# Spreading the weight rounding of a fused HGRN2 and serf-MLP kernel: load order, rounding rate and activation steps of the first turns

## The chip, the cores and the metric

The kernel runs on one core of a Trainium2 chip. The metric is the device time of one execution in microseconds, the median of three runs. The profile is of one execution of the same program. Engines are named as in the profile: PE is TensorE, DVE VectorE, ACT ScalarE, POOL GpSimd, SP the engine that issues most of the DMAs.

## The reference

The first part is a gated linear recurrence over 768 time steps for 4 batches and 8 heads of width 48. The second part is a two-layer MLP over the 3072 tokens, with the activation h * erf(softplus(h)).

```python
f = 1.0 / (1.0 + np.exp(-f_logit))
for t in range(S):                       # S = 768
    state = f[:, :, t, :, None] * state + np.einsum('bhd,bhe->bhde', k[:, :, t], v[:, :, t])
    y[:, :, t] = np.einsum('bhd,bhde->bhe', q[:, :, t], state)
x = y.transpose(0, 2, 1, 3).reshape(B * S, H * D)      # 3072 x 384
h = x @ w_in                                           # 384 x 2048
sp = np.maximum(h, 0.0) + np.log1p(np.exp(-np.abs(h)))
out = (h * erf(sp)) @ w_out                            # 2048 x 384
```

The two weight matrices come as 64-bit floats; everything else is 32-bit.

## The kernel before

**Tiling.** The sequence is cut into 24 chunks of 128 time steps (6 for each batch), and two chunks make a block of 256 tokens, so there are 12 blocks. A chunk `g` goes through four stages. `stage_d` (L381) sums the log decays with one matmul, takes two exponentials on ACT, sends eight small DMAs that put the chunk's total decays into `Tall` (L398, from chunk 3 on), and scales q and k on DVE into `qd` and `kd` (L402, L406). `stage_t` (L410) transposes both on PE and copies them out of PSUM on ACT, and releases the state update that the chunk before had left over (`late`). `stage_s` (L450) makes the scores and the state products on PE, masks the scores (on DVE for chunks 0 to 2, L503; on ACT and POOL from chunk 3 to 9, L495 and L498) and updates the state on DVE (`next_state`, L443 to L446). `stage_y` (L511) forms the output of the chunk on PE and copies it on ACT into `xT`, the input of the MLP (L536). `clamp` (L357, DVE) and `logs` (L363, ACT) prepare a block's decays ahead of its `stage_d`; `prepare` is both in a row.

**MLP.** `hidden(blk, gi)` (L585) makes one of four groups of 512 hidden columns of a block: 12 steps of one fp32 matmul each, which PE carries out as two, and one eviction on ACT (L601). `activate` (L546) is a generator of ten steps for each group. Step 1 is an exponential, 2 and 3 are two tanh (all ACT), 4 and 5 two products on DVE (L165), then three empty steps, 9 a last tanh (ACT, L566), 10 a product (DVE, L568). `act_step` (L574) advances each running group by one step and starts the next group five steps after the one before, so that two run at once. The tiles `e` and `x` have two buffers each. `project_first` (L673) and `project` (L701) are the second matmul; the later one uses seven products in place of eight, with sums made on DVE (`sum_w`, `sum_h`).

**Rounding.** The 64-bit weights are loaded raw in 16 pieces of 768 KB, eight of `w_in` and eight of `w_out`, into places that are still free: `w_out_sb`, the ring `Hg` of hidden groups, and `scratch` (`HOMES`, L264). `round_piece` (L295) turns a piece into 32-bit floats with one ACT operation (L311) and six DVE operations (L313, L317, L322, L326, L331, L336). `weights_step` (L851) issues one DVE operation of the piece in work; the ACT operation of the next piece goes out ahead of L331. So a piece takes six steps. `load_more` (L868) loads a further piece of `w_out` when the piece that had its place before has been rounded. A matmul with a piece's weights waits for that piece's L336: `hidden(blk, gi)` needs pieces 2 gi and 2 gi + 1.

**Order of the work.** The order on every engine is written out by hand (`tc.manual_schedule`): each engine carries out its instructions in the order in which the program issues them. A front part (L819 to L919) brings chunks 0 and 1 through all stages and chunk 2 through the first two. Then come 12 turns (`for it in range(n_blocks)`, L937). A turn has slots: in each slot `slots(it)` issues one matmul step of the MLP, and the loop body adds to it what is due. These are rounding steps from the accumulator `due` (L955), a further load (L959), a stage of the recurrence when the slot is in the list `at` (L961), clamp and logs of a later block, and an activation step (L984 to L995). Turn 1 (`it == 0`) has 96 slots: the hidden groups of blocks 0 and 1, in the order of block and group 0.0, 0.1, 1.0, 0.2, 1.1, 0.3, 1.2, 1.3. Turn 2 has 48 slots (block 2). Turn 3 has 80 (block 3, then the second matmul of block 0). Turn 4 begins with the second matmul of block 1.

```python
due += (1 if s < 42 else 0.6 if s < 72 else 0.3) if it == 0 else 0.42 if it == 1 else 0.6
while due >= 1:
    weights_step()
    due -= 1
```

Of the kernel before, what the change touches and what calls it, by code (L numbers as in the profile page):

```python
# [74 lines left out]
def kernel(  # L75
# [21 lines left out]
    CPB = 2  # L97
# [131 lines left out]
    def load(g, what="qkv", queue=None):  # L229
        b, c = divmod(g, NCH)  # L230
        queue = queue or nc.sync
        for src, t, n in ((q, qns[g % NQ], "q"), (k, kns[g % NQ], "k")):
            if n in what:
                queue.dma_start(out=t[:].rearrange("t (h d) -> t h d", d=D), in_=heads(src, b, c))
        if "v" in what:
            queue.dma_start(
                out=vts[g % NV][:].rearrange("t (h d) -> t h d", d=D), in_=heads(v, b, c)
            )
# [40 lines left out]
    def load_piece(i):  # L279

        assert home_free(i)
        n = d_ff // n_pieces
        if i < n_pieces:
            dst = w_in_sb[:, :, bass.ts(i, n)]
        else:
            m = n_ft // n_pieces
            j = i - n_pieces
            dst = w_out_sb[:, bass.ts(j, m), :]
        raw = None if wpe == 1 else raw_home(i).bitcast(U32)
        to = dst if wpe == 1 else raw.rearrange("p (t w) -> p t w", t=dst.shape[1])  # L290
        src = w_in[:, bass.ts(i, n * wpe)] if i < n_pieces else w_out[bass.ts(j, m * P), :]
        nc.sync.dma_start(out=to, in_=src.rearrange("(t p) w -> p t w", p=P))
        raws[i] = (dst, raw)
# [63 lines left out]
    def clamp(blk, j0, j1):  # L357
        lt = lts[blk][:, j0:j1, :].rearrange("t j c -> t (j c)")
        nc.vector.tensor_scalar(
            out=lt, in0=lt, scalar1=LOGIT_MIN, scalar2=None, op0=ALU.max  # L360
        )

    def logs(blk, j0, j1):  # L363

        lt = lts[blk][:, j0:j1, :].rearrange("t j c -> t (j c)")
        use_exp_ln()
        nc.scalar.activation(out=lt, in_=lt, func=AF.Exp, scale=-1.0)
        nc.scalar.activation(out=lt, in_=lt, func=AF.Ln, bias=1.0)

    def prepare(*which):  # L370
        clamp(*which)
        logs(*which)
# [444 lines left out]
    with tc.manual_schedule():  # L817
# [5 lines left out]
        load(0, "kv", nc.scalar)  # L823
        load(0, "q")
        load_f(1)
        load(1, "qk")
        load_f(2)
        load_piece(0)
        load(1, "v")
        load(2)  # L830
        load_piece(1)
        load_piece(2)
        load_f(3)
        nc.gpsimd.memset(tri[:], 1.0)
# [45 lines left out]
        def weights_steps(n):  # L880
            for _ in range(n):
                weights_step()
# [5 lines left out]
        keep_busy(6)  # L888
        prepare(0, 1, 2)
        stage_t(0)  # L890
        load(3, "qk")
        load_piece(3)
        stage_d(1)
# [42 lines left out]
        due = 0.0  # L936
        for it in range(n_blocks):  # L937
            gen, n = slots(it)
            if it == 0:
                todo = [(stage_s, 2), (stage_y, 2), (stage_d, 3), (stage_t, 3), (stage_s, 3), (stage_y, 3),  # L940
                        (stage_d, 4), (stage_t, 4), (stage_d, 5), (stage_s, 4), (stage_t, 5),
                        (stage_y, 4)] + stages(2)[4:]
                at = [1, 5, 6, 12, 16, 23, 34, 42, 48, 52, 60, 74, 76, 80, 88, 94]
            else:
                todo = stages(it + 2) if it + 2 < n_blocks else []
                at = [n * x // 48 for x in (2, 6, 11, 17, 25, 29, 34, 41)] if it == 1 else [int(3 + (n - 13) / max(1, len(todo)) * i) for i in range(len(todo))]
            if ADJACENT <= it + 2 < n_blocks:

                at = [0, 1, 15, 24, 31, 52, 66] if it + 2 == ADJACENT else [2, 26, 42, 54, 76, 90]
                at = at[: len(todo)]  # L950
            if it + 3 < n_blocks:
                prepare_at = at[todo.index((stage_d, (it + 3) * CPB))] - 14
            at, todo = deque(at), deque(todo)
            for s, _ in enumerate(gen):
                due += (1 if s < 42 else 0.6 if s < 72 else 0.3) if it == 0 else 0.42 if it == 1 else 0.6  # L955
                while due >= 1:
                    weights_step()
                    due -= 1
                if s % 6 == 3:  # L959
                    load_more()  # L960
                if at and s == at[0]:  # L961
                    at.popleft()
                    f, g = todo.popleft()
                    f(g)
                    if f in (stage_y, stage_y_s):
                        if g + NSV < n_chunks:
                            load_sv(g + NSV)
                        load_to(g + LOOK)
                        if g == 2:
                            load(5, "v")  # L970
                            load_piece(7)
                if it == 0 and s == 14:
                    prepare(2, 0, CPB)
                if it == 0 and s == 9:
                    load_f(6)
                    load_f(7)
                if s == n // 2 and it + 4 < n_blocks:
                    for j in range(CPB):
                        load_f((it + 4) * CPB + j)
                if it + 3 < n_blocks and s == prepare_at - 6:  # L980
                    clamp(it + 3, 0, CPB)
                if it + 3 < n_blocks and s == prepare_at:
                    logs(it + 3, 0, CPB)
                if it < 2:  # L984
                    step = it == 1 and s % 6 == 3
                elif it == 2:
                    step = s % 5 in (1, 3)
                elif it == 3:
                    step = s % 7 in (1, 4)
                elif it == n_blocks - 1:  # L990
                    step = s % 3 == 1
                else:
                    step = s % 9 in (2, 6)
                if step:
                    act_step()  # L995
                if it == 2:
                    if s % 2:
                        sum_step()
                elif it > 2:
                    if s == n - n_h and it < n_blocks - 1:  # L1000
                        to_sum.extend(sum_h(groups[it - 1, gi]) for gi in range(NS))
                    if it == n_blocks - 1 and s % n_o == 40 and s < 2 * n_o:
                        blk = n_blocks - 2 + s // n_o
                        to_sum.extend(sum_h(groups[blk, gi]) for gi in range(NS))
                    if it == 3:
                        if s % 2:
                            sum_step()
                    elif s < n_o or s % 3 == 0 or it == n_blocks - 1:
                        sum_step()
                if it == n_blocks - 2 and s in (5, 40):  # L1010
                    next(check)
            assert not todo
# [214 lines left out]
```

## Time and profile before

| | before |
|---|---|
| time, median of 3 (lowest to highest) | 618.1 us (617.54 to 618.85) |
| profiled span | 616.6 us |
| PE busy | 588.3 us (95%) |
| weight loads on PE | 514.5 us (83%) |
| DVE busy | 459.7 us (75%) |
| ACT busy | 382.9 us (62%) |
| POOL busy | 14.9 us (2%) |
| mean granted PE clock | 0.985 |
| HBM read, written | 35.59 MB, 4.72 MB |

The table of stages, the chain of waits and the timelines are read in the prediction. In the timeline a line gives the start, the duration from the first start to the last end, engine, line, operation and tiles, the number of instructions merged into it, and in brackets how long the engine was idle before it and what released it. In the list of waits a line names who waited, for whom, how many us in total, how many times, and the longest. A busy PE is not PE at its peak, since the ends of matmuls are modelled and the clock varies; the granted clock stands beside it in the table of stages.

### The profile page before, as it was taken

The numbers are of one execution on the slowest core, as the hardware profiler recorded it, in microseconds if no ns is written. First come the engines' busy times: TensorE is split into PE (matmuls) and PEld (weight loads), VectorE is DVE, ScalarE is ACT, GpSimd is POOL, SyncE is SP. The second block draws the span as 40 slices with busy tenths as digits, with TensorE's granted clock in tenths as the row PEclk, the third lists the DMA queues.
The fourth block names the chain that finished last, engine by engine and source line by source line (L and its number), as shares of the span: only waits on it lengthen the run. The fifth ranks groups of instructions, "written<-read, shape, count | busy, mean of one in ns | idle before, by whom it ended". The sixth has DMA issues, their size and how long they took to land.

```text
span 616.6 us, 13769 instructions
## 1 busy us (share of the span) xinstructions
PE 588.3 (95%) x5729; PEld 514.5 (83%) x5729; DVE 459.7 (75%) x785; ACT 382.9 (62%) x483; POOL 14.9 (2%) x33
## 2 busy tenths in 40 slices
PE   8778799999999999999999999999999999999996
PEld 7556688887655689989989988988988989989996
DVE  4898998697489597896896875896886795656651
ACT  5735365987875678875866585875775666366000
POOL 1000011010000000000000000000000000000000
PEclk9987899999999999999999999999999999999999
DMA  9998753441241222133133132042130000000000
GB/s 201 248 228 208 199 175 63 71 88 17 53 77 28 41 63 52 25 81 54 33 71 53 32 73 53 14 91 53 15 65 15 3 27 0 28 1 0 27 27 30
DMA packets 155604, 41.36 MB, mean 67 GB/s; under 512 B 147344, under 2 KB 150416, under 8 KB 155536
## 3 DMA queue, kind: packets, MB, share of 16 engines
q1 hardware_dynamic: 153312, 39.82, 29.6%
q8 instruction: 47, 0.77, 0.5%
q10 hardware_dynamic: 2224, 0.59, 0.4%
q14 instruction: 21, 0.17, 0.1%
HBM read 35.59 MB, written 4.72 MB: 65 GB/s over the span
## 4 chain that ended last, share of the span: by engine, by line
PE 74%; DVE 11%; ACT 8%; DMA 3%; issue 2%; SPq 1%; POOL 0%; DVEq 0%; ACTq 0%; POOLq 0%
PE hps L594 31%; PE ops L735 25%; PE ops L684 7%; PE y L532 3%; PE ps_t L418 3%; PE ps_d L387 2%; ACT x L160 2%; PE sc L467 1%; PE sc L475 1%; DVE sv L445 1%; DVE sv L446 1%; DVE w_in_sb L322 1%; DVE Hg L568 1%; DVE w_in_sb L336 1%; PE busy L379 1%
## 5 line engine op out<-in xcount | busy, mean ns | idle before, releaser
L594 PE MATMUL hps<-xT,w_in_sb 128*128 128x256 f32 x1152 | 264.7, 386 | 5.0 <-DVE w_in_sb L336 2.9
L594 PEld LDWEIGHTS hps<-xT,w_in_sb 128*128 128x128 f32 x1152 | 218.5, 193 | 39.2 <-ACT xT L536 2.8
L165 DVE SCALAR_TENSOR_TENSOR e<-x,e 128x1024 f32<-128x1024 f32 x96 | 117.1, 1220 | 13.2 <-ACT x L160 12.6
L160 ACT ACTIVATE x<-Hg,serf_bias 128x1024 f32<-128x1024 f32 x88 | 97.5, 1140 | 0.2
L157 ACT ACTIVATE e<-Hg 128x1024 f32<-128x1024 f32 x44 | 46.5, 1058 | 61.7 <-DVE Hg L568 57.6
L735 PE MATMUL ops<-wT,Hg 128*128 128x192 f32 x320 | 78.4, 328 | 0.0
L568 DVE TENSOR_TENSOR Hg<-Hg,e 128x1024 f32<-128x1024 f32 x44 | 53.7, 1222 | 22.6 <-ACT e L566 22.5
L735 PE MATMUL ops<-wT,scratch 128*128 128x192 f32 x288 | 67.8, 326 | 0.9 <-DVE scratch L743 0.9
L735 PE MATMUL ops<-w_out_sb,Hg 128*128 128x192 f32 x320 | 65.1, 326 | 0.0
L601 ACT COPY Hg<-hps 128x1024 f32<-128x1024 f32 x44 | 44.4, 1010 | 32.7 <-PE hps L594 32.4
L735 PEld LDWEIGHTS ops<-wT,Hg 128*128 128x128 f32 x320 | 55.7, 190 | 1.9
L735 PEld LDWEIGHTS ops<-w_out_sb,Hg 128*128 128x128 f32 x320 | 54.6, 190 | 2.0
L566 ACT ACTIVATE e<-e 128x1024 f32<-128x1024 f32 x48 | 50.3, 1048 | 1.9 <-DVE e L165 1.8
L735 PEld LDWEIGHTS ops<-wT,scratch 128*128 128x128 f32 x288 | 50.2, 190 | 1.1 <-issue 1.1
L503 DVE TENSOR_TENSOR qA<-sc,tri 64x256 f32<-64x256 f32 x68 | 28.7, 422 | 27.3 <-PE sc L475 26.3
L743 DVE TENSOR_TENSOR scratch<-scratch,ops 128x384 f32<-128x384 f32 (+1 forms) x41 | 20.3, 494 | 29.5 <-ACT scratch L751 23.0
L532 PEld LDWEIGHTS y<-qA,sv 128*32 128x32 f32 x1536 | 24.9, 113 | 19.6 <-issue 12.4
L532 PE MATMUL y<-qA,sv 128*32 128x64 f32 x1536 | 29.9, 226 | 10.9 <-issue 5.1
L425 ACT COPY qA<-ps_t 64x512 f32<-64x512 f32 x48 | 27.7, 577 | 19.4 <-PE ps_t L418 19.0
L402 DVE TENSOR_TENSOR qd<-qn,dp 128x384 f32<-128x384 f32 x24 | 13.4, 556 | 33.6 <-ACT dp L390 33.5
L735 PE MATMUL ops<-w_out_sb,scratch 128*128 128x192 f32 x144 | 34.7, 326 | 0.0
L445 DVE TENSOR_TENSOR sv<-sc,sv 48x192 f32<-48x192 f32 x80 | 28.3, 354 | 8.3 <-ACT qA L495 6.9
(111 smaller groups left out, 648.1 us busy)
## 6 DMA issues: line engine op xcount, KB each, us to landing
lt<-in_f_logit_dram SPq DMA_DIRECT2D x24, 192.0 KB, 3.7
qn<-in_q_dram SPq DMA_DIRECT2D x24, 192.0 KB, 3.4
kn<-in_k_dram SPq DMA_DIRECT2D x23, 192.0 KB, 3.7
vt<-in_v_dram SPq DMA_DIRECT2D x23, 192.0 KB, 3.7
out_dram<-scratch SPq DMA_DIRECT2D x11, 384.0 KB, 2.6
sv<-in_v_dram SPq DMA_DIRECT2D x84, 48.0 KB, 2.8
w_out_sb<-in_moe_w_in_dram SPq DMA_DIRECT2D x4, 768.0 KB, 6.1
Hg<-in_moe_w_in_dram SPq DMA_DIRECT2D x4, 768.0 KB, 6.6
```

Of the source, the lines that this page charges most:

```text
L157: nc.scalar.activation(out=dst[:], in_=h, func=AF.Exp)
L160: nc.scalar.activation(out=dst[:], in_=h, func=AF.Tanh, bias=serf_bias[:, i : i + 1], scale=SERF_KAB[i][0])
L165: nc.vector.scalar_tensor_tensor(out=e[:], in0=x[:], scalar=SERF_KAB[i][2], in1=e[:], op0=ALU.add, op1=ALU.mult)
L445: nc.vector.tensor_tensor(out=new, in0=add, in1=old, op=ALU.add)
L503: nc.vector.tensor_tensor(out=qA[half(1 - r), r, :, half(c)], in0=sc[half(c), r], in1=tri1[half(c)].unsqueeze(1).broadcast_to((C, HP, C)), ...
L532: nc.tensor.matmul(y[M * i : M * (i + 1), kt, half(c)], lhsT=sv[:, r, c, a, o : o + M], rhs=qA[:, r, a, half(c)], start=(n == 0), stop=Tru ...
L566: nc.scalar.activation(out=e[:], in_=e[:], func=AF.Tanh, scale=SERF_C)
L568: nc.vector.tensor_tensor(out=h, in0=h, in1=e[:], op=ALU.mult)
L594: nc.tensor.matmul(hps[:, j, :], lhsT=w_in_sb[:, kt, ft * P : (ft + 1) * P], rhs=xTs[blk][:, kt, :], start=(kt == 0), stop=(kt == n_k - 1),)
L601: nc.scalar.copy(out=gr["h"], in_=hps[:])
L684: nc.tensor.matmul(ops[:, tt, 0:d_model], lhsT=gr["h"][:, j, tt * P : (tt + 1) * P], rhs=w_out_sb[:, ft, :], start=(ft == 0), stop=(ft == ...
L735: nc.tensor.matmul(place[n], lhsT=x[:, j, :], rhs=y, start=(gi == 0 and j == 0 and n in first), stop=(gi == n_g - 1 and j == 1), skip_grou ...
```

## The change

Five edits, all in the order of the work; no operation is added or removed.

- The first piece of `w_in` is loaded ahead of q, k and v of chunk 1, and piece 1 ahead of chunk 2.
- Two rounding steps are issued right after `stage_t(0)`, so that the front has 12 steps where it had 10.
- The rounding rate follows what is needed next: 1 step a slot only to slot 18 of turn 1, then 0.46, then 0.3; 0.65 in turn 2, 0.45 after it. The last steps fall into turn 3.
- Pieces of `w_out` are asked for in every second slot where it was every sixth.
- Activation steps: three in turn 1 (slots 77, 85, 93) and nine in turn 2, where there were none and eight; in turn 3, 23 of its 80 slots where it was 32. In turn 1 `stage_d(3)` goes ahead of `stage_y(2)`, `stage_d(4)` and `stage_t(4)` move by two slots and one, and clamp and logs of block 2 move from slot 14 to slots 18 and 24.

It is for taking rounding out of DVE's way in turn 1, where the weights are rounded long before a matmul wants them, and for evening out the activation work over the first three turns.

```diff
         load(0, "q")
         load_f(1)
-        load(1, "qk")
+        load_piece(0)
+        load(1, "qkv")
         load_f(2)
-        load_piece(0)
-        load(1, "v")
+        load_piece(1)
         load(2)
-        load_piece(1)
         load_piece(2)
         load_f(3)
...
         stage_t(0)
+        weights_steps(2)
         load(3, "qk")
...
             if it == 0:
-                todo = [(stage_s, 2), (stage_y, 2), (stage_d, 3), (stage_t, 3), (stage_s, 3), (stage_y, 3),
+                todo = [(stage_s, 2), (stage_d, 3), (stage_y, 2), (stage_t, 3), (stage_s, 3), (stage_y, 3),
                         (stage_d, 4), (stage_t, 4), (stage_d, 5), (stage_s, 4), (stage_t, 5),
                         (stage_y, 4)] + stages(2)[4:]
-                at = [1, 5, 6, 12, 16, 23, 34, 42, 48, 52, 60, 74, 76, 80, 88, 94]
+                at = [1, 5, 8, 12, 16, 23, 36, 43, 48, 52, 60, 74, 76, 80, 88, 94]
...
-                due += (1 if s < 42 else 0.6 if s < 72 else 0.3) if it == 0 else 0.42 if it == 1 else 0.6
+                due += (1 if s < 18 else 0.46 if s < 66 else 0.3) if it == 0 else 0.65 if it == 1 else 0.45
...
-                if s % 6 == 3:
+                if s % 2:
                     load_more()
...
-                if it == 0 and s == 14:
-                    prepare(2, 0, CPB)
+                if it == 0 and s == 18:
+                    clamp(2, 0, CPB)
+                if it == 0 and s == 24:
+                    logs(2, 0, CPB)
...
-                if it < 2:
-                    step = it == 1 and s % 6 == 3
-                elif it == 2:
-                    step = s % 5 in (1, 3)
-                elif it == 3:
+                if it == 0:
+                    step = s >= 72 and s % 8 == 5
+                elif it == 1:
+                    step = s % 5 == 3
+                elif it < 4:
                     step = s % 7 in (1, 4)
```

## The prediction

> **What bounds the kernel now.** I read the table of stages first, cut at the ends of the turns as TensorE's timeline shows them. Turn 1 (`it == 0`) runs from its first `hps` matmul at 28.3 us to 105.6 us, turn 2 to 135.2, turn 3 to 189.6; everything after is the fourth and later turns. The columns are TensorE, weight loads, VectorE, ScalarE, GpSimd (busy us and instructions), granted clock, DMA share, GB/s.
>
> ```profile
> 28.30:57.90 29.60, 23.11 (x322) 17.65 (x322) 26.55 (x49) 13.05 (x22) 1.31 (x2) 0.85 0.83 203
> 57.90:77.50 19.60, 16.39 (x61) 13.65 (x62) 18.92 (x29) 7.07 (x11) 0.00 (x0) 0.81 0.81 213
> 77.50:105.60 28.10, 28.10 (x355) 23.39 (x353) 26.93 (x44) 16.88 (x29) 4.25 (x6) 1.00 0.48 124
> 105.60:135.20 29.60, 29.18 (x374) 24.47 (x374) 21.24 (x37) 26.91 (x39) 3.15 (x4) 1.00 0.42 73
> 135.20:189.60 54.40, 50.49 (x437) 36.27 (x437) 39.60 (x57) 42.43 (x52) 2.99 (x4) 1.00 0.28 50
> 189.60:616.60 427.00, 419.91 (x3828) 380.67 (x3826) 307.76 (x528) 257.92 (x295) 1.01 (x4) 1.00 0.19 38
> ```
>
> TensorE is the bound from 77.5 us on: no gap up to 105.6, 4.3 us of gaps in turns 2 and 3 together, and 7.1 us in the remaining 427, most of them in the last drain. Before 77.5 it is not. From 28.3 to 77.5 it is idle 9.7 us and its clock is 0.81 to 0.85, while VectorE is 90 and then 97% busy. The chain of work that ended last says the same; here it is just before 77.5 (start us, us, what):
>
> ```profile
> 69.59 0.48 DVE w_in_sb L313
> 70.09 0.57 DVE w_in_sb L317
> 70.69 0.96 DVE w_in_sb L322
> 71.65 0.48 DVE qd L402
> 72.26 1.88 PE ps_t L418 x8
> ```
>
> Rounding (L313 to L336) stands in VectorE's queue ahead of the `qd` that TensorE's transposes want. TensorE's timeline around it:
>
> ```profile
> 57.95 7.05 PE L594 MATMUL hps<-xT,w_in_sb 128*128 128x256 f32 x22 [0.57 <-ACT xT L536]
> 65.48 3.62 PE L594 MATMUL hps<-xT,w_in_sb 128*128 128x256 f32 x16
> 72.26 1.03 PE L418 MATMUL ps_t<-ident,qd 128*128 128x128 f32 x4 [3.16 <-DVE qd L402]
> 73.93 3.66 PE L594 MATMUL hps<-xT,w_in_sb 128*128 128x256 f32 x12
> 80.88 3.72 PE L594 MATMUL hps<-xT,w_in_sb 128*128 128x256 f32 x16
> ```
>
> A full-speed matmul takes 3.65/16 = 0.23 us, so a slot (two matmuls) takes 0.46. After a pause it takes 0.32 (at 57.95) or 0.30 (at 73.93). Each pause is paid twice: as a wait, and as a slow restart. In turns 2 and 3 the waits are of another kind (waiter, releaser, us in total, times, longest):
>
> ```profile
> ACT e L157 <- DVE wT L568: 7.8, 4, 2.4
> PE y L532 <- issue: 3.3, 3, 1.5
> DVE w_out_sb L313 <- ACT w_out_sb L311: 3.0, 1, 3.0
> ```
>
> ScalarE's queue stalls at the exponential of an activation group until VectorE has finished the group two before (two `e` buffers), and the copies queued behind it hold up `y` (0.42, 1.37 and 1.51 us, at 116, 151 and 176 us). The other waits of those turns are ScalarE evictions, 0.61 and 0.42.
>
> **What the skill says.** The Trainium skill, "TensorE: Matmul & The Clock Gate" (Part 1): the array runs at half clock by default, goes back to it after an idle window of about 3.4 us, and needs about as long of sustained work to recover. The trace agrees with the halving: in slices of 2 us the clock is 0.50 from 56 to 62 and 0.56 to 0.59 from 72 to 76; but it also falls after several shorter waits together (1.69, 0.41 and 0.57 us), and not after the single ones of 1.37 and 1.51. "VectorE: DVE Perf Modes" (The perf-mode tier table): fp32 tensor_scalar runs at 2x, tensor_tensor at 1x. The trace agrees: 0.56 us against 0.96 for the same 768 elements. "DMA: Bandwidth & Descriptors" (Queues, rings and completion order): descriptors on a ring are consumed in order, so what is put ahead delays what follows; the trace of before cannot show the new order.
>
> **The change, part by part.** *Price of a step.* A piece costs six steps. One piece runs from 74.96 to 79.62 on VectorE: 4.66 us, 0.777 a step. There are 16 pieces, 96 steps, before and after. Nothing is removed; 74.6 us of rounding only move.
>
> *Count.* Before: 10 steps ahead of turn 1, 42 + 0.6 x 30 + 0.3 x 24 = 67 in it, 19 in turn 2. After: 12 ahead, 18 + 0.46 x 48 + 0.3 x 30 = 49 in turn 1, 0.65 x 48 = 31 in turn 2, and the last 4 in the first nine slots of turn 3. Turn 1 loses 18 steps, 14 us; turn 2 gains 12, turn 3 gains 4.
>
> *Front.* The first two steps now stand ahead of `stage_d(1)`. By 5, 10 and 15 us the queues had moved about 0.70, 1.75 and 3.02 MB (139, 211 and 253 GB/s). With piece 0 (0.79 MB) ahead, chunk 1's q and k are complete at 2.16 MB, about 11.6 us, instead of 1.38 MB. VectorE wants them after the two roundings. Those wait for the Abs (0.9 us) behind ScalarE's `kT` copy, which ended at 12.2, so `qd` starts at about 14.1 instead of 12.63. The data are there: no cost from DMA. The queue work is then 1.3 us later until the state update of chunk 1, which ends at 27.5 instead of 26.2. `y(1)`, its copy and the first `hps` follow it: 29.2 instead of 28.3. Turn 1 no longer starts on a wait for L336, but gains nothing there. VectorE carries two steps more by then.
>
> *Slots 0 to 23.* The stage that releases the second block's `y(3)` is the state update of `stage_s(3)`, slot 16. VectorE reached it at 52.37 and then waited 1.85 us for ScalarE's `sc` copies, which were behind the logs of block 2. Now clamp and logs come after it. VectorE has 12 + 17 = 29 steps ahead of it instead of 27 (L326 and L331, 1.53 us) and the clamp of 0.47 no longer, so it gets there at 53.4 and ends its four operations at 54.9. Before it ended at 56.2. `y(3)` before waited for GpSimd as well and ended at 57.4; I expect 56.3, between 55.9 (full clock) and 57.0 (half clock). **Gain 1.1 us.** Moving `stage_d(3)` ahead of `stage_y(2)` starts the `Tall` transfers earlier; they had landed in time anyway.
>
> *Slots 24 to 48.* `qd` of `stage_d(4)` had 45 steps ahead of it (slot 34) and has 38 now (slot 36): 5.4 us less work, 71.65 - 5.4 = 66.2. TensorE, 1.1 us earlier and one slot later, reaches the transposes at 68.5. So the **3.16 us wait** goes, and with it the half clock after it. Over 73.93 to 77.5 and the eight transposes ahead (1.88 instead of 0.87) that cost 0.9 + 1.0: **1.9 us**. The half clock after `y(3)`, 58 to 62 us, I leave in place, since shorter waits remain ahead of it (2.1 us lost, as before). Total for turn 1: 1.1 + 3.2 + 1.9 = **6.2 us**. After slot 48 TensorE was gapless before and VectorE is emptier now: nothing more.
>
> *Turns 2 and 3.* VectorE's work in turn 2, in the order of its queue: 31 steps 24.1, two `stage_d` and the states 7.2, a clamp 0.5, five activation operations of 1.14 (start to start) 5.7: 37.5 us. TensorE needs 48 x 0.46 + 7.0 = 29.1. Backlog 8.4 us at the end of turn 2. It does not fall on TensorE whole, since each stage is asked for some ten slots after it was queued. `y(7)` at slot 41 needs the state queued at slot 29: 24.4 us of VectorE work against 25.4 us on TensorE, so no wait. `xT` of chunk 7, behind a blocked exponential on ScalarE: 1.0 us. `y(8)`, slot 28 of turn 3, has a worse place. Its PSUM slot waits for ScalarE's copies of slot 19, behind the exponential of slot 11, behind the multiply of slot 8. Counted from turn 3's start, that multiply ends at 37.5 + 4 x 0.777 + 0.9 + 1.14 + 1.2 - 29.1 = 14.8; the exponential, two tanh and the copy add 4.6, so 19.4 us, where TensorE arrives at 15.9: 3.5 us, less the 1.0 just paid. The last steps of turn 3 have nine activation steps less on both engines (23 instead of 32); of the waits there (0.61, 0.42, 1.51) I leave 1. Slot 72, where the last group of block 0 is forced to finish, may cost 0.5, and a start of turn 2 with VectorE idle 0.5. Sum 1.0 + 2.5 + 1.0 + 1.0 = 5.5 against 4.3 now: **loss 1.2 us**. Its bounds are 1 (all of it hidden but the first term) and 8.4 plus a half-clock restart.
>
> *At nothing.* w_out loaded sooner: its rounding order and rates come 14 slots or more after the load, and DMA runs at 0.42 of its share in turn 2. Activation steps in turn 1: three, all on ScalarE, which is 60% busy there. One table load moves from turn 2 into turn 1 (1.28 us in the trace). Turn 4 starts three activation steps behind and catches up by forcing two; TensorE has work there.
>
> **Rivals.** *Pushed, not hidden* (slower): the 8.4 us of backlog reach TensorE whole in turn 3 and bring a restart at half clock (1.9), in place of the waits at 116 and 151 us (1.8): 618.1 - 6.2 + 8.4 - 1.8 + 1.9 = 620.4. For it: ScalarE's exponential resynchronises with VectorE every five steps. Against: VectorE has 8.4 and 14.8 us free in turns 2 and 3. *More relief*: no half clock after `y(3)` (2.1) and no waits left late in turn 3 (2.5): 618.1 - 6.2 - 2.1 - 2.5 = 607.3. *Late front*: chunk 1 comes 3.4 us late (0.79 MB at 230 GB/s) and the whole front shifts: 613.1 + 3.4 = 616.5; against it, the data have 2.5 us in hand.
>
> **The numbers.** Likeliest: 618.1 - 6.2 + 1.2 = 613.1, chance 0.54; more relief 0.20; late front 0.12; pushed 0.14. The range from 607.0 to 618.4 takes in the first three and leaves out most of the fourth. Faster by over 0.2% (below 616.9): 0.53 + 0.20 + 0.06 = 0.79; within 0.2%: 0.08; slower: 0.13.
>
> **What would show it.** Right: no wait of TensorE for `qd` L402, slot 48 about 6 us earlier, VectorE over 95% busy in turn 2, a `y` wait of some 3 us early in turn 3. Wrong: first `hps` after 30 us (late front), clock under 1.00 in turn 3 (pushed), clock 1.00 all through turn 1 (more relief).

## The result, and the profile after

The changed kernel takes 628.7 us (median of 4 runs, 625.6 to 629.6); the kernel before took 618.1 in the same comparison (617.5 to 618.9). The ratio is 1.0161, with a 95% interval from 1.0124 to 1.0198. It is 10.5 us slower, where 613.1 us, a gain of 5.0, was forecast. The forecast was wrong in its sign.

The table of stages of the changed kernel is cut, like the one of before, at the ends of its own turns: turn 1 is the first three rows, then turn 2, turn 3, the first 32 slots of turn 4, and the rest. The columns are stretch and length, TensorE, weight loads, VectorE, ScalarE, GpSimd (busy us and instructions), granted clock, DMA share, GB/s.

```profile
27.90:55.80 27.90, 21.13 (x322) 15.81 (x322) 26.68 (x48) 11.41 (x20) 1.96 (x2) 0.94 0.82 208
55.80:70.00 14.20, 14.20 (x61) 12.08 (x62) 12.35 (x21) 7.24 (x11) 0.00 (x0) 0.88 1.03 287
70.00:98.20 28.20, 28.20 (x355) 23.39 (x353) 20.61 (x36) 20.78 (x33) 3.26 (x6) 1.00 0.54 136
98.20:128.70 30.50, 29.55 (x373) 24.09 (x372) 26.63 (x40) 23.87 (x36) 4.01 (x4) 1.00 0.41 72
128.70:187.90 59.20, 52.23 (x438) 37.52 (x438) 46.83 (x70) 40.33 (x51) 4.10 (x4) 0.97 0.25 46
187.90:222.30 34.40, 29.81 (x250) 18.27 (x250) 18.22 (x33) 15.83 (x18) 0.51 (x2) 0.85 0.17 36
222.30:626.50 404.20, 394.64 (x3578) 364.85 (x3576) 290.66 (x495) 244.20 (x279) 0.50 (x2) 1.00 0.18 37
```

Turn 1 does what was hoped. Its second row stood at 19.6 us with 3.2 us of idle TensorE and is 14.2 without a gap now. Turn 1 ends at 98.2 instead of 105.6. Then it is given back: turn 3 is 59.2 us long instead of 54.4, and the stretch after it has 4.6 us of idle TensorE and a clock of 0.85. In the kernel before, that stretch had neither:

```profile
189.60:215.00 25.40, 25.40 (x252) 15.82 (x251) 18.39 (x34) 15.62 (x18) 0.50 (x2) 1.00 0.17 35
```

TensorE's list of waits in the changed kernel, its two costliest lines (waiter, releaser, us in total, times, longest):

```profile
PE y L532 <- issue: 6.2, 3, 3.9
PE ops L684 <- DVE Hg L568: 4.6, 1, 4.6
```

The wait for `qd` (3.16 us) has gone from the list. The second line is new: the second matmul of the MLP waits for the last product of an activation group.

To see where time goes I use the sum matmul of `stage_d` (`ps_d`, L387) as a mark. It stands at a fixed slot: chunk 6 at slot 76 of turn 1, chunk 9 at slot 3 of turn 3, 11 and 12 at slots 1 and 31 of turn 4, 13 at slot 2 of turn 5. The work between two marks is nearly the same in both kernels, so the differences show where time was won and lost (all from TensorE's timeline, of one execution of each kernel).

| stretch | before, us | after, us | difference |
|---|---|---|---|
| start to chunk 6 | 93.45 | 85.92 | -7.5 |
| 6 to 9 (end of turn 1, turn 2) | 43.30 | 46.42 | +3.1 |
| 9 to 11 (turn 3) | 55.16 | 57.86 | +2.7 |
| 11 to 12 (start of turn 4) | 23.07 | 32.14 | +9.1 |
| 12 to 13 (rest of turn 4) | 25.43 | 26.68 | +1.2 |
| 13 to the end | 376.2 | 377.5 | +1.3 |

The last 1.3 us lie behind TensorE's last matmul, which ends 8.6 us later than before (620.0 us instead of 611.4), so in the final copies and stores. The start of turn 4 is the largest loss. The chain of work that ended last shows what is in it (start us, us, what):

```profile
201.76 1.15 ACT x L160
...
202.93 1.28 ACT L347
...
204.23 0.85 ACT lt L367
...
205.10 0.84 ACT lt L368
...
205.97 1.28 ACT L160
...
207.26 1.15 ACT x L160
208.41 0.96 ACT e L566
...
209.39 1.24 DVE Hg L568
...
210.66 1.65 PE ops L684 x2
```

ScalarE has the two tanh of block 2's first group and then the last tanh of block 1's group 3 to do. Between the two tanh stand the logs of block 6, with a table load ahead of them (L347) and one after them (L160): 1.28 + 0.85 + 0.84 + 1.28 = 4.25 us. VectorE's product for group 3 of block 1 comes after that, and TensorE's next matmul wants that group. By the program's order, the kernel before issues this last tanh at slot 11 of turn 4 and the product at slot 15, both ahead of the logs at slot 17; the changed kernel issues them at slots 22 and 24, behind the logs. The restart is slow; TensorE's timeline, in the changed kernel:

```profile
210.66 1.65 PE L684 MATMUL ops<-w_out_sb,Hg 128*128 128x384 f32 x2 [4.59 <-DVE Hg L568]
...
215.79 6.71 PE L684 MATMUL ops<-w_out_sb,Hg 128*128 128x384 f32 x14
```

The last line has 0.48 us a matmul. In the kernel before, 14 of the same took 0.34 each:

```profile
210.36 4.78 PE L684 MATMUL ops<-w_out_sb,Hg 128*128 128x384 f32 x14
```

In the changed kernel the clock is 0.50 in every slice of 2 us from 210 to 218.

### The profile page after: what moved, and what is told of

Read it like the earlier page. It is cut to its first block, busy times and chain, and to the rows that moved or that the text cites. A ratio compares the mean times of both kernels' runs of the same rounds, so it can differ in the third digit from the quotient of the medians.

```text
span 626.5 us, 13759 instructions
## 1 busy us (share of the span) xinstructions
PE 591.7 (94%) x5729; PEld 514.7 (82%) x5729; DVE 461.5 (74%) x785; ACT 382.2 (61%) x483; POOL 16.5 (3%) x33
## 4 chain that ended last, share of the span: by engine, by line
PE 72%; ACT 11%; DVE 10%; DMA 2%; issue 2%; SPq 2%; ACTq 0%; DVEq 0%
PE hps L594 30%; PE ops L735 25%; PE ops L684 6%; PE y L532 3%; ACT x L160 3%; PE ps_t L418 2%; PE ps_d L387 2%; PE sc L475 1%; PE sc L467 1%; DVE Hg L568 1%; SPq L254 1%; ACT e L566 1%; ACT e L157 1%; DMA qn<-in_q_dram 1%; ACT qA L425 1%
## 5 line engine op out<-in xcount | busy, mean ns | idle before, releaser
L160 ACT ACTIVATE x<-Hg,serf_bias 128x1024 f32<-128x1024 f32 x88 | 97.6, 1140 | 0.2
L568 DVE TENSOR_TENSOR Hg<-Hg,e 128x1024 f32<-128x1024 f32 x44 | 53.8, 1222 | 24.6 <-ACT e L566 24.4
```

Of the source, the lines that this page charges most:

```text
L160: nc.scalar.activation(out=dst[:], in_=h, func=AF.Tanh, bias=serf_bias[:, i : i + 1], scale=SERF_KAB[i][0])
L568: nc.vector.tensor_tensor(out=h, in0=h, in1=e[:], op=ALU.mult)
```

## The experiments

Theory A: the loss is made in turn 4 by the activation schedule. Theory B: the rounding pushed into turn 2 makes it, and late activation is its shadow. After the first four runs two more theories were put: C, that the changed rates win in slots 18 to 43 only and lose by what they push into turn 2; D, that any rounding after slot 43 costs turn 1. The medians and ratios are each against the kernel before in the same comparison, at 618.0 to 618.3 us. The marks of all runs are in a table at the end of this section.

**Turn 3's activation rate of before.**

```diff
-                elif it < 4:
+                elif it == 2:
+                    step = s % 5 in (1, 3)
+                elif it == 3:
                     step = s % 7 in (1, 4)
```

> The changed kernel with the activation rate of before in turn 3 alone (32 of 80 slots in place of 23). Theory A (the loss is made in turn 4: the last group of block 1 is forced to finish behind ScalarE's table swap for the logs, 4.6 us of wait and some 4.5 us of half clock): that group is done before slot 24 of turn 4, no wait there, 628.7 - 9 = about 620, with the 4 us wait for y early in turn 3 still there. Theory B (the backlog of rounding in turn 2 is the cause, and the late activation only its shadow): more activation on the same backlog makes turn 3's waits longer, 627 or more.

Measured 617.1 us, ratio 0.9993 (0.9981 to 1.0004). The start of turn 4 takes 23.07 us, to the hundredth what it took before, and no wait stands in it. So 11.6 us of the changed kernel's time hang on the nine activation steps fewer in turn 3. The wait early in turn 3 is there, in two parts (TensorE's timeline):

```profile
146.24 4.11 PE L594 MATMUL hps<-xT,w_in_sb 128*128 128x256 f32 x10 [2.21 <-ACT Hg L601]
152.05 1.21 PE L532 MATMUL y<-qA,sv 128*32 128x64 f32 x64 [1.70 <-issue]
```

**The logs of block 6 earlier.** Clamp and logs go to slots 2 and 8 of turn 4; the activation steps stay as changed.

```diff
                 prepare_at = at[todo.index((stage_d, (it + 3) * CPB))] - 14
+                if it == 3:
+                    prepare_at = 8
```

> The changed kernel with clamp and logs of block 6 in turn 4 moved from slots 11 and 17 to slots 2 and 8; activation rates as changed. Theory A: the table swap and the logs (1.28 + 1.7 + 1.28 us) are out of the way of the last tanh, the wait at slot 24 of turn 4 falls from 4.6 to under 1.5 us and the half clock after it goes: 619 to 622. Theory B: the activation is late whatever stands beside it, the wait stays over 3 us: 626 or more.

Measured 620.4 us, ratio 1.0048 (1.0030 to 1.0066): 8.3 us faster than the changed kernel. The wait at slot 24 is 1.43 us and there is no half clock after it. ScalarE's timeline shows the same work with the logs out of the way:

```profile
194.75 0.84 ACT L367 ACTIVATE lt<-lt 128x768 f32<-128x768 f32 x1
...
201.29 1.28 ACT L160 ACT_TABLE_LOAD   x1
...
204.68 1.04 ACT L566 ACTIVATE e<-e 128x1024 f32<-128x1024 f32 x1
```

The last tanh starts at 204.68 instead of 208.31, with as few activation steps as in the changed kernel. The steps being late is one condition, the logs in between the other. Giving the steps back removes the loss in turn 4 whole; moving the logs removes most of it, and 2.9 of 10.3 us stay (24.77 and 26.67 us between the marks, instead of 23.07 and 25.43). The Trainium skill, "ScalarE: Activation LUTs" (What ACT_TABLE_LOAD costs), gives about 1283 ns for a load and about 1380 more for a drain at every switch. The traces here show the 1.28 us; between either load of the changed kernel's turn 4 and the activations on both sides of it lie at most 0.03 us, and a drain is not seen.

**The rounding rates of before** in the changed kernel.

```diff
-                due += (1 if s < 18 else 0.46 if s < 66 else 0.3) if it == 0 else 0.65 if it == 1 else 0.45
+                due += (1 if s < 42 else 0.6 if s < 72 else 0.3) if it == 0 else 0.42 if it == 1 else 0.6
```

> The changed kernel with the rounding rates of before (1, 0.6, 0.3; 0.42; 0.6); front, load order, stage slots and activation steps as changed. Theory A: turn 1 loses its gain of some 6 us again and turn 4's wait stays: 630 or more, with turns 2 and 3 about 4 us better, so 628 to 633. Theory B: the waits of turns 2 to 4 go with the backlog: 617 to 621.

Measured 622.6 us, ratio 1.0079 (1.0062 to 1.0095), between the two. Turn 4's wait is the same to the hundredth, with no backlog of rounding at all:

```profile
208.49 1.65 PE L684 MATMUL ops<-w_out_sb,Hg 128*128 128x384 f32 x2 [4.59 <-DVE Hg L568]
```

So theory B is wrong on turn 4. It has a point on the rest: without the changed rates the stretch from chunk 6 to 11 is 94.3 us instead of 104.3. With the same activation steps in both kernels, the changed rates win 7.8 us ahead of chunk 6 and lose 10.0 from there to chunk 11.

**The activation steps alone**, on the kernel before.

```diff
-                if it < 2:
-                    step = it == 1 and s % 6 == 3
-                elif it == 2:
-                    step = s % 5 in (1, 3)
-                elif it == 3:
+                if it == 0:
+                    step = s >= 72 and s % 8 == 5
+                elif it == 1:
+                    step = s % 5 == 3
+                elif it < 4:
                     step = s % 7 in (1, 4)
```

> The kernel before with the changed activation steps alone (3, 9, 23 in the first three turns). Theory A: turn 4's wait at slot 24 and its half clock appear here too, 618.1 + 8 = 626, less a little for turn 3's shorter waits: 623 to 627. Theory B: no backlog, so no wait: 616 to 619.

Measured 622.0 us, ratio 1.0070 (1.0053 to 1.0087); I had expected 623 to 627. Turn 4's wait of 4.59 us is here too. But the steps also win: from chunk 9 to 11 the kernel takes 51.2 us instead of 55.2, since TensorE's waits there fall from 3.9 us to 1.0. That was more than I allowed for.

**Rates that use the slack of turn 1.** In the changed kernel VectorE is busy 20.6 of 28.2 us from 70.0 on. This run puts rounding back there and lowers turn 2's rate.

```diff
-                due += (1 if s < 18 else 0.46 if s < 66 else 0.3) if it == 0 else 0.65 if it == 1 else 0.45
+                due += (1 if s < 18 else 0.46 if s < 43 else 0.62) if it == 0 else 0.42 if it == 1 else 0.45
```

> The changed kernel with other rounding rates: as changed to slot 43 of turn 1, then 0.62 in place of 0.46 and 0.3, and 0.42 in place of 0.65 in turn 2, so that some 13 steps come back into slots 43 to 95 of turn 1, where VectorE was idle about 10 us. Activation steps as changed. Theory C (turn 1's gain comes from slots 18 to 43 alone, and what costs in turns 2 and 3 is the rounding pushed into turn 2): turn 1 still ends some 7 us early, the waits of 1.8 us for xT and 3.9 us for y early in turn 3 fall to under 1 us together, turn 4's wait of 4.6 us stays: 628.7 - 10 = 617 to 620. Rival D (any rounding after slot 43 delays TensorE in turn 1 as it did before): turn 1 ends 3 us or more later than in the changed kernel, 622 or more.

Measured 620.4 us, ratio 1.0039 (1.0023 to 1.0055), just above what C expects (617 to 620). Chunk 6 to 9 takes 43.7 us instead of 46.4, and 9 to 11 53.8 instead of 57.9: the pushed rounding had cost 6.8 us there. Chunk 6 is 2.1 us later than in the changed kernel. The rates are not the reason: the next run has them and has chunk 6 at 85.90 us. The run after it has them too, and chunk 6 at 88.12. In that trace and in this one the first `hps` starts 0.9 to 1.0 us later and TensorE's clock is at half from about 28 to 38 us; in the changed kernel and the next run it is at half for 3.4 us there. Rival D falls with the next run.

**The same rates, and turn 3's activation rate of before from slot 40 on.**

```diff
-                elif it < 4:
+                elif it == 2:
+                    step = s % 7 in (1, 4) if s < 40 else s % 5 in (1, 3)
+                elif it == 3:
                     step = s % 7 in (1, 4)
```

> The same rates, and in turn 3 the activation rate of before from slot 40 on (28 steps in turn 3, so 40 by its end as in the kernel before), the changed rate ahead of slot 40. Theories A and C together: no wait at slot 24 of turn 4, turn 3's waits gone, turn 1 about 7 us better: 618 - 7 - 3 = 606 to 610. If the waits of turn 3 came from the number of activation steps and not from where they stand, they come back: 612 or more.

Measured 608.8 us, ratio 0.9841 (0.9824 to 0.9858): 9.4 us faster than the kernel before and 19.9 faster than the changed one. Chunk 6 is at 85.90, and turn 4 takes 23.07 and 25.43 us as before. Its trace is of the slowest of its four executions (610.9 us). The intent of the change holds; its rounding rates from slot 43 of turn 1 on and its activation rate late in turn 3 do not.

**The same rates with the logs of block 6 early**, in place of the later activation steps.

```diff
-                due += (1 if s < 18 else 0.46 if s < 66 else 0.3) if it == 0 else 0.65 if it == 1 else 0.45
+                due += (1 if s < 18 else 0.46 if s < 43 else 0.62) if it == 0 else 0.42 if it == 1 else 0.45
...
                 prepare_at = at[todo.index((stage_d, (it + 3) * CPB))] - 14
+                if it == 3:
+                    prepare_at = 8
```

> The same rates with the changed activation steps, and clamp and logs of block 6 at slots 2 and 8 of turn 4. Theories A and C: like the kernel with these rates alone less 7 to 8 us for turn 4's wait and its half clock: 609 to 613.

Measured 615.0 us, ratio 0.9951 (0.9932 to 0.9971). I expected 609 to 613. It is 5.3 us better than with the logs at their old place. In turn 4, 1.42 us at slot 24 and 1.18 at the next `y` remain, and its marks add 2.9 us to those of before. Early logs are the poorer cure, though 2.2 us of the distance to the run above lie ahead of chunk 6 and do not come from the logs.

**The front alone**, on the kernel before: the new load order and the two rounding steps ahead of chunk 1.

```diff
         load_f(1)
-        load(1, "qk")
+        load_piece(0)
+        load(1, "qkv")
         load_f(2)
-        load_piece(0)
-        load(1, "v")
+        load_piece(1)
         load(2)
-        load_piece(1)
         load_piece(2)
...
         stage_t(0)
+        weights_steps(2)
```

> The kernel before with the changed load order and the two rounding steps ahead of chunk 1's stage alone. My prediction gave this nothing by itself: 617 to 619. If the late chunk 1 cost time, 620 or more; if the earlier piece helped turn 1's start, 616 or less.

Measured 620.6 us, ratio 1.0038 (1.0025 to 1.0050). It costs 2.3 us, where the prediction had nothing. The first `hps` matmul is no later (28.11 us). What is later is `y(3)`; the kernel before and then this run:

```profile
54.57 0.31 PE L532 MATMUL y<-qA,sv 128*32 128x64 f32 x4 [1.69 <-POOL qA L498]
...
55.66 0.31 PE L532 MATMUL y<-qA,sv 128*32 128x64 f32 x4 [3.72 <-POOL qA L498]
```

The clamp on VectorE comes only 0.3 us later (50.66 us instead of 50.35). But the Abs of the next piece (L311, 0.87 us), which stood behind the scores' copies in ScalarE's queue, now stands ahead of them, since it goes out with the rounding steps. So the copies, GpSimd's selects (54.95 instead of 53.86) and `y(3)` are 1.1 us later. Chunk 6 is 1.3 us later; where the rest comes from is not shown. In the whole change the clamp and the logs stand behind `y(3)`, so the cost need not arise there; the next run tries that. The load order and the two steps were not tried apart.

**The last rates with the front of before.** The two steps come in turn 1 (rate 1 to slot 20).

```diff
-        load_piece(0)
-        load(1, "qkv")
+        load(1, "qk")
         load_f(2)
-        load_piece(1)
+        load_piece(0)
+        load(1, "v")
         load(2)
+        load_piece(1)
...
         stage_t(0)
-        weights_steps(2)
...
-                due += (1 if s < 18 else 0.46 if s < 43 else 0.62) if it == 0 else 0.42 if it == 1 else 0.45
+                due += (1 if s < 20 else 0.46 if s < 43 else 0.62) if it == 0 else 0.42 if it == 1 else 0.45
```

> The kernel with the rates that use turn 1's slack and the later activation in turn 3 (608.8 us), with the front of before: its load order, and 10 rounding steps there instead of 12, so that rate 1 goes on to slot 20 instead of 18. The front edit alone cost 2.3 us on the kernel before. If that cost is the front's own, 606 to 607.5; if it came from that kernel's crowded turn 1, where it pushed GpSimd's selects for chunk 3 later, it is not there to be won back: 608 to 610.

Measured 607.3 us, ratio 0.9838 (0.9809 to 0.9866), 1.6% faster than the kernel before and the lowest median of all. The interval of the kernel it started from (0.9824 to 0.9858) lies within this one, so the comparison does not tell whether the front matters in that setting.

**The rates alone**, on the kernel before.

```diff
-                due += (1 if s < 42 else 0.6 if s < 72 else 0.3) if it == 0 else 0.42 if it == 1 else 0.6
+                due += (1 if s < 18 else 0.46 if s < 66 else 0.3) if it == 0 else 0.65 if it == 1 else 0.45
```

> The kernel before with the changed rounding rates alone. My prediction: 6.2 us won in turn 1 and 1.2 lost, 613. As the traces since read (7.5 won by the end of turn 1, waits early in turn 3 and ScalarE's backlog giving most of it back, no wait in turn 4 since the activation steps are those of before): 615 to 618. Theory B (the pushed rounding is what makes the changed kernel slow): 622 or more.

Measured 626.2 us, ratio 1.0131 (1.0096 to 1.0165). This is theory B's figure, and I had not expected it. ScalarE's timeline and then TensorE's, early in turn 3:

```profile
147.34 1.06 ACT L157 ACTIVATE e<-Hg 128x1024 f32<-128x1024 f32 x1 [8.41 <-DVE wT L568]
...
157.18 1.06 ACT L157 ACTIVATE e<-wT 128x1024 f32<-128x1024 f32 x1 [3.31 <-DVE wT L568]
```

```profile
150.39 2.43 PE L594 MATMUL hps<-xT,w_in_sb 128*128 128x256 f32 x10 [1.68 <-ACT Hg L601]
159.52 2.05 PE L532 MATMUL y<-qA,sv 128*32 128x64 f32 x64 [6.71 <-issue]
```

ScalarE stands 8.4 us before its exponential, since the product that frees the buffer is behind the rounding in VectorE's queue: VectorE has worked without a gap since 122.3 us when it reaches that product at 146.0. An eviction behind the exponential holds TensorE up for 1.7 us. The `y` waits 6.7 more, because the copies ahead of it stand behind the next exponential, which waits for VectorE again. Then the `y` runs at half clock. Turn 1 wins only 2.6 us, since with the old stage slots and ten steps ahead the rounding comes too late for a `w_in` piece (2.35 us of wait for L336 at 83 us, and a restart at half clock). So the rates alone follow the rival "pushed, not hidden", and do worse than its 620.4.

**The stage slots alone**, with the split of clamp and logs.

```diff
-                todo = [(stage_s, 2), (stage_y, 2), (stage_d, 3), (stage_t, 3), (stage_s, 3), (stage_y, 3),
+                todo = [(stage_s, 2), (stage_d, 3), (stage_y, 2), (stage_t, 3), (stage_s, 3), (stage_y, 3),
...
-                at = [1, 5, 6, 12, 16, 23, 34, 42, 48, 52, 60, 74, 76, 80, 88, 94]
+                at = [1, 5, 8, 12, 16, 23, 36, 43, 48, 52, 60, 74, 76, 80, 88, 94]
...
-                if it == 0 and s == 14:
-                    prepare(2, 0, CPB)
+                if it == 0 and s == 18:
+                    clamp(2, 0, CPB)
+                if it == 0 and s == 24:
+                    logs(2, 0, CPB)
```

> The kernel before with the moved stage slots of turn 1 and the split of clamp and logs alone. The scores of chunk 3 no longer stand behind the logs on ScalarE, so GpSimd's selects come some 4 us sooner and the wait of 1.7 us for them goes: turn 1 ends 1 to 2 us sooner, 616 to 617.5. If the rounding in VectorE's queue is the only bound there: 618.

Measured 617.3 us, ratio 0.9987 (0.9978 to 0.9997): a small gain, as expected. The wait for GpSimd is gone and chunk 4's mark is 4.7 us earlier (60.09 us instead of 64.84). Most of that is lost again at the next wait, the one for `qd`:

```profile
70.92 1.08 PE L418 MATMUL ps_t<-ident,qd 128*128 128x128 f32 x4 [7.00 <-DVE qd L402]
```

It was 3.16 us before. Chunk 5's mark is only 1.8 us earlier. Without fewer rounding steps ahead of `qd`, most of the earlier `y(3)` is waited away.

**TensorE kept busy in turn 4's wait.** The changed kernel, with extra matmuls that take the place of nothing.

```diff
+                if it == 3 and s == 23:
+                    warm = ps_at.tile([P, 512], FP32, name="warm", tag="at")[:, 0:P]
+                    for _ in range(16):
+                        nc.tensor.matmul(warm, lhsT=tri[:], rhs=tri[:], start=True, stop=True)
```

> The changed kernel with 16 matmuls of the triangle on itself, whose sums nobody reads, queued on TensorE ahead of slot 24 of turn 4: about 3.7 us of work inside the wait of 4.6. If the rest of turn 4's loss is the half clock after the wait, that goes and the wait itself stays: 628.7 - 4 = 623 to 625.5. If slower instructions than that have another cause, no change: 628 or more.

Measured 624.5 us, ratio 1.0110 (1.0082 to 1.0137): 4.1 us faster than the changed kernel for more work. The wait ends at the same distance from the mark of chunk 11 (20.5 us in both), and what follows runs at full clock:

```profile
206.23 3.73 PE L1001 MATMUL warm<-tri 128*128 128x128 f32 x32
210.99 0.91 PE L684 MATMUL ops<-w_out_sb,Hg 128*128 128x384 f32 x2 [1.02 <-DVE Hg L568]
...
213.83 4.78 PE L684 MATMUL ops<-w_out_sb,Hg 128*128 128x384 f32 x14
```

So of the 9.1 us lost at the start of turn 4, 4.6 are the wait and 4.2 the half clock after it (32.14 against 27.93 us between the marks). It agrees with the Trainium skill, "TensorE: Matmul & The Clock Gate" (Part 1), in that idling halves the clock and busy work keeps it. For the recovery the page has one window or more of about 3.4 us of sustained work. In the changed kernel TensorE worked from 210.66 without a gap, and the clock came back only near 219.7 (0.57 on average from 218 to 220). Counted from where the clock had fallen, near 209.5, it was at half for 10.2 us, three times 3.4. After the same wait it was one or two times 3.4 us in other kernels (last section), so the 4.2 us are the price in this trace and not a fixed one.

**The rates with the earlier activation steps of turns 1 and 2** (three and nine), turn 3 as before.

```diff
-                if it < 2:
-                    step = it == 1 and s % 6 == 3
+                if it == 0:
+                    step = s >= 72 and s % 8 == 5
+                elif it == 1:
+                    step = s % 5 == 3
```

> The kernel before with the changed rounding rates and the changed activation steps of turns 1 and 2 (three and nine); turn 3 keeps its 32 steps. With the rates alone it took 626.2 us, with a wait of 6.7 us for y in turn 3. If what matters is where ScalarE's exponential stands against the backlog, the three earlier steps bring that wait to under 3 us, as in the changed kernel with turn 3's old rate (617.1): 617 to 621. If the backlog on VectorE alone decides, the wait stays over 5 us: 624 or more.

Measured 621.9 us, ratio 1.0073 (1.0051 to 1.0096), just outside what either reading expects. The two waits are 2.19 and 3.40 us, 5.6 together, against 8.4 with the rates alone and 3.9 in the first experiment. Earlier activation steps help, but the backlog costs by itself. What makes up the rest of the 4.8 us to the first experiment I did not separate; that kernel has the front and the stage slots of the change besides, and no wait for a `w_in` piece at 82 us, which is 2.36 us here. In this trace, the fastest of its four executions, the clock is also at half for 17 us between 26 and 51 us, and in the trace of the first experiment not at all.

**The slack rates alone**, on the kernel before.

```diff
-                due += (1 if s < 42 else 0.6 if s < 72 else 0.3) if it == 0 else 0.42 if it == 1 else 0.6
+                due += (1 if s < 20 else 0.46 if s < 43 else 0.62) if it == 0 else 0.42 if it == 1 else 0.45
```

> The kernel before with rates that use turn 1's slack (1 to slot 20, 0.46 to slot 43, then 0.62; 0.42; 0.45) and nothing else. If pushing rounding out of turn 1 is what cost 8 us with the changed rates, and lowering it in slots 20 to 43 is what wins: turn 1 ends 4 to 6 us sooner, no wait over 2 us in turn 3, 612 to 615. If any lower rate in turn 1 comes back as a wait later: 619 or more.

Measured 613.6 us, ratio 0.9949 (0.9917 to 0.9980). Turn 1 is won with the old front and the old stage slots (chunk 6 at 85.81), and 2.8 us of it are lost from there to chunk 11: the `y` of turn 3 still waits 3.37 us, where I expected under 2. A better turn 1 needs both, no backlog in turn 2 and an activation schedule that leaves ScalarE room in turn 3.

The marks of every run, in us, each from one execution (the time is the median of all):

| | to chunk 6 | 6 to 9 | 9 to 11 | 11 to 12 | 12 to 13 | time |
|---|---|---|---|---|---|---|
| before | 93.45 | 43.30 | 55.16 | 23.07 | 25.43 | 618.1 |
| changed | 85.92 | 46.42 | 57.86 | 32.14 | 26.68 | 628.7 |
| turn 3's old activation | 86.08 | 46.44 | 58.21 | 23.07 | 25.43 | 617.1 |
| logs early | 85.47 | 46.43 | 57.83 | 24.77 | 26.67 | 620.4 |
| old rates | 93.75 | 43.05 | 51.22 | 30.15 | 26.68 | 622.6 |
| activation alone | 93.48 | 43.49 | 51.22 | 29.47 | 26.67 | 622.0 |
| slack rates | 88.05 | 43.67 | 53.81 | 29.30 | 26.68 | 620.4 |
| slack rates, later activation | 85.90 | 44.65 | 53.05 | 23.07 | 25.43 | 608.8 |
| slack rates, logs early | 88.12 | 43.68 | 54.30 | 24.77 | 26.67 | 615.0 |
| front alone | 94.71 | 44.11 | 55.07 | 23.07 | 25.43 | 620.6 |
| slack rates, later activation, old front | 84.28 | 43.92 | 53.28 | 23.07 | 25.43 | 607.3 |
| rates alone | 90.82 | 46.39 | 62.43 | 23.07 | 25.43 | 626.2 |
| stage slots alone | 91.67 | 43.28 | 55.13 | 23.07 | 25.43 | 617.3 |
| kept busy | 86.05 | 46.40 | 58.07 | 27.93 | 26.67 | 624.5 |
| rates, early activation | 88.09 | 45.53 | 59.05 | 23.08 | 25.43 | 621.9 |
| slack rates alone | 85.81 | 44.13 | 57.15 | 23.07 | 25.43 | 613.6 |

The fourth and fifth columns take three kinds of values only. They are 23.07 and 25.43 where activation was as far on at the end of turn 3 as before, or further; 24.77 and 26.67 with the logs early; and 27.9 to 32.1 with 26.7 in the others, where the wait is the same (filled in one case) and the half clock differs.

Put alone on the kernel before, the rates cost 8.2 us, the activation steps 4.1 and the front 2.3, and the stage slots win 0.8. Taken back from the changed kernel, turn 3's activation rate is worth 11.6 us and the rates 6.1. The two orders differ because the parts act on each other's waits, so no single part can be called the cause of the whole 10.5 us. What is shown is where each loses: the activation steps in turn 4, the rates in turns 2 and 3.

## Why the prediction was wrong

**Turn 1: right, its size in part by luck.** The wait for `qd` is gone and so is the half clock behind it. `y(3)` ended at 55.2 us (56.3 forecast). The half clock after it stayed, as assumed (26 matmuls in 7.57 us), but it lasted 3.4 us where it had lasted 6.8. That is about 1.7 us that the forecast did not count on, and no run shows that the change is the reason. By the mark of chunk 6 the gain is 7.5 us, with 6.2 forecast.

**Front: right in the whole, wrong alone.** In the changed kernel the first `hps` starts at 27.99 us, where 29.2 was forecast (28.31 before): `qd` of chunk 1 started at 13.2 us and not at 14.1, so chunk 1 had its data in time. That the two early steps can cost 2.3 us further on, through ScalarE's queue and GpSimd, I had not seen.

**Turns 2 and 3: the mechanism was right, the term too small.** The forecast loss was 1.2 us; the marks show 5.8. `y(8)` waited 3.93 us (3.5 forecast), for the reason given: ScalarE's exponential waits for VectorE, and the copies behind it end just before the `y` starts.

```profile
145.82 1.06 ACT L157 ACTIVATE e<-wT 128x1024 f32<-128x1024 f32 x1 [6.63 <-DVE wT L568]
...
148.97 1.17 ACT L425 COPY qA<-ps_t 64x512 f32<-64x512 f32 x2
150.24 1.21 PE L532 MATMUL y<-qA,sv 128*32 128x64 f32 x64 [3.93 <-issue]
```

`xT` of chunk 7 took 1.80 (1.0), slot 72 took 0.99 (0.5), and a slow restart after `y(8)` came on top, 14 matmuls in 4.97 us instead of 3.29: 1.7 us that I had put only at the bound. All waits between chunks 6 and 11 come to 7.8 us, with 5.5 forecast. The runs also show that two effects stand behind the 5.8 us. The pushed rounding cost about 10 us there (104.3 us instead of 94.3 with the new activation steps, 108.8 instead of 98.5 with the old), and the new activation steps won some 4 back (94.3 and 94.7 instead of 98.5). So the step by which the backlog of 8.4 us "does not fall on TensorE whole" did not hold in sum: the rates cost as much there as the whole backlog with a slow restart. The marker I named, VectorE over 95% busy in turn 2, was off as well: it was 26.6 of 30.5 us, 87%, because it waits for ScalarE in turn (3.1 us for `dp`).

**Turn 4: the step that failed.** The prediction costed it at nothing: "Turn 4 starts three activation steps behind and catches up by forcing two; TensorE has work there." It cost 9.1 us, and 1.2 more at the next `y`. By the program's order one step is forced in turn 4, not two. It is the last of a group whose matmul is the next in TensorE's queue, so there was no other work. I counted steps, but did not write out ScalarE's queue at that place, where the logs and two table loads stood, 4.25 us. Nor did I add the half clock, although a 3 us wait had shown it in the trace of before. With turn 4 at its old length the changed kernel would be at about 618, near the 617.1 us of the first experiment. So turn 4 decides the sign, but without it, too, the forecast gain of 5 us would not have come: turns 2 and 3 had used it up.

**The rivals.** "Pushed, not hidden" named the right side and the right place for the rates, and its backlog of 8.4 us with a restart of 1.9 comes near the 10 us that they cost there in sum. Its sign, a clock under 1.00 in turn 3, came too (0.97). In the whole change about a third of what is lost behind chunk 6 is of its kind. No rival had turn 4 in it, so its 620.4 is too low as well.

Not tried by itself: the denser asking for `w_out` pieces. No wait for one of them shows in TensorE's list of waits.

## What to carry to other kernels

When an edit makes a background job later, find the point where someone is forced to finish it, and write out each engine's queue at that point, not the count of steps: what stands ahead of the last step is paid in full. Work taken out of a crowded stage should go into the nearest stage with slack, here the second half of the same turn, rather than to the latest allowed moment: on the kernel before, the first took 613.6 us and the second 626.2. A long wait on TensorE costs more than its length. The 4.6 us of turn 4 cost 6.2 to 9.1 us in four kernels, so such a wait is worth filling.

## What the runs showed of the hardware

**How long the half clock lasts.** With the granted clock read in slices of 0.5 us and each moment taken as either full or half, the start and the end of every half-clock time can be worked out. Between 6 and 260 us the sixteen traces have 48 of them, and every one lasts 3.4, 6.8 or 10.2 us: one, two or three times 3.41. After the same wait of 4.6 us in turn 4 it was 3.4 us with the slack rates and with the activation steps alone, 6.8 with the old rates and 10.2 in the changed kernel. The stretch from chunk 11 to 12 took 29.30, 29.47, 30.15 and 32.14 us. What decides between one, two and three is not shown. Differences of two microseconds between single executions can come from that alone.

**VectorE beside GpSimd.** Single-operand operations of VectorE took 1.02 and 0.89 us instead of 0.56 while GpSimd's selects ran (the L313 at 48.42 and the L317 at 49.48 of the changed kernel, with selects from 47.92 to 49.95).
